# The first eleven stretches of an attention kernel in another written order, and its end with P V ahead of the output projection

## The chip, the cores and the metric

The kernel runs on one core of one Trainium2 chip, in one launch. The metric is the device time of one execution in microseconds: the median of 3 runs was 817.11 us before the change (814.79 to 817.4). A core has a matrix engine (TensorE, "PE" in the profile, its weight loads "PEld"), a vector engine (VectorE, "DVE"), a scalar engine for activations (ScalarE, "ACT"), a slower general engine (GpSimd, "POOL") and a queue that issues transfers (SyncE, "SP"). Each runs its own instructions in the order in which they were written; semaphores hold an instruction until what it reads is there and what it overwrites is free.

## The reference

```python
W = min(4096, max(256, Sk // 4))                                   # 512
q = (xn @ wq).reshape(B, Sq, Hq, Dh).transpose(0, 2, 1, 3)         # 2048 rows, 32 heads of 192
k = k_cache[:, :, Sk - W:, :];  v = v_cache[:, :, Sk - W:, :]
p = softmax(einsum("bhqd,bhkd->bhqk", q, k) * Dh ** -0.5)
s = einsum("bhqk,bhkd->bhqd", p, v).transpose(0, 2, 1, 3).reshape(B, Sq, Hq * Dh) @ wo
r = xn @ w_r;  idx = argsort(-r)[:, :2]                            # two tokens
y = (silu(x_sel @ w_gate) * (x_sel @ w_up)) @ w_down * sigmoid(r_sel)
g = silu(xn + scatter(y at idx))
return x + s * g                                                   # xn = layernorm(x), bfloat16
```

x is 2048 x 640, so 16 tiles of 128 rows. Nearly all the arithmetic is attention over the last 512 keys and the two projections around it; the feed-forward part touches two rows.

## The kernel before

The 32 heads go in 8 groups of 4, a group in two pairs of heads. A step i is one group, one block of 512 rows (t5, four tiles) and one pair: 64 steps, written i = 8g + 2·t5 + pair. A unit n is one tile of 128 rows of a step, n = 4i + u, so 256 units. Units are worked on in "stretches": stretches 0 and 1 have two units each, all others three, 86 in all (line 89).

What one stretch does is a list of tokens, read by `first` (line 636), each writing a few instructions:

- `S.j` (`scores`, L305 and L312): twelve matmuls into six PSUM tiles `sc`, two heads for each unit. The pool `ps_p` has six such buffers, so all of the last stretch's must be free.
- `M.n.h` (`row_max`, L320): the row maximum on DVE. `E.n.h` (`exps`, L327): the exponential on ScalarE, with the row sum. `P.n` (`p_turn`, L332): a transposing transfer of the probabilities, issued by SP.
- `q.i.c` (`q_mul`, L291): one of three 128-column parts of q for step i, five matmuls that read the turned activations `xnT` and the weights `wq_p` into a buffer of the pool `ps_f` (two buffers). `qe` (`q_out`, L281 on DVE or L283 on ScalarE) scales it out of PSUM. With a range of tiles behind it (`q.0.0.2.4`) only these rows are done.
- `R.j`, `O.n`, `OO.n.m`, `Oe.n` and `T.j`: for the stretch before, the reciprocal of the row sums, P V (`o_mul`, L346; in `ps_f` for `O`, in `ps_p` for `OO`), its scaling out of PSUM (`o_out`, L361 on DVE, L359 on ScalarE) and the transposing transfer of the result (`o_turn`, L367).
- `W.w` (`w_mul`, L394): the output projection of one tile of 128 rows for one group, twelve matmuls in two halves of 320 columns, from `oT` and `wo_g`, into two buffers of `ps_p`. `We.w` (`w_out`, L398 on) adds it to the sum `s_acc`; for the last group it multiplies by the gate and adds the rest (`fin_t`, L413 and `fin_o`, L415 or L419), and stores the tile. `OT.n` (`o_turn_pe`, L370 on) turns P V on TensorE in place of a transfer.
- Loads: `x` (x_in), `wq`, `k`, `kT` (a transposing transfer of k), `v`, `wo`. A trailing `a`, `v` or `g` names the engine (ScalarE, DVE, GpSimd); without one the transfer is issued by SP. (Where a range of tiles stands behind the letter, as in `qe.0.1.v.0.2`, the letter is not read and ScalarE does it.)
- Layer norm of a tile: `bn` (statistics on DVE) or `as` (the same on ScalarE, L223 and L224, with a small step on GpSimd), `rs.lo.hi.q` (the reciprocal root for tiles lo to hi in twelve Newton steps on DVE, L174 to L204) or `rg.lo.hi` (the same from the third step on GpSimd, fourteen steps, L191 to L210), `ap` (applying it), `turn` (turning on TensorE, copied out) or `xT.lo.hi` (a transposing transfer into `xnT`, L252).
- `B.j.k`: what the background plan has put into slot k of stretch j: the loads of later groups, the feed-forward part, the loads for the end.

The first ten stretches are written out by hand in the string `FIRST` (line 815), in which tokens of several stretches are mixed; stretches 10 to 84 come from `stretch(j)` (line 787) and the last from the string `LAST` (line 834). The scores of a stretch need q of its units: units 8 to 11 belong to step 2, which is the first to read tiles 4 to 7; step 4 reads tiles 8 to 11, step 6 tiles 12 to 15. The loads for the groups from 1 on are put by `at` (lines 719 to 732) a fixed number of units ahead of the group's first unit. A tile's buffer is reused in the order of the written release, and a transfer also waits until the one eight places earlier has landed.

## Time and profile before

| what | value |
|---|---|
| median of 3 runs | 817.11 us (814.79, 817.11, 817.4) |
| the profiled execution | 814.84 us |
| its span in the profile | 813.1 us |
| TensorE busy | 786.6 us (97%), 5742 matmuls |
| DVE busy | 630.7 us (78%) |
| ScalarE busy | 480.7 us (59%) |
| GpSimd busy | 168.1 us (21%) |
| data moved by transfers | 143.80 MB, mean 177 GB/s |
| mean granted TensorE clock | 0.992 |

The profile is of one execution. A row of a timeline has the start and the length of a run of like instructions, the engine, the line, the operation and its tiles, the count, and in brackets the idle time of that engine just before and what ended it. A row of the windows has the busy time of each engine within a stretch of time, the clock that TensorE was granted (1.00 is full), and what the 16 DMA engines did.

### The profile page before, as it was taken

How to read it: one execution, taken by the hardware profiler on the slowest of the kernel's cores; microseconds unless marked ns; L12 is line 12 of the kernel's file. 1: busy time of each engine (PE TensorE's matmuls, PEld its weight loads, DVE VectorE, ACT ScalarE, POOL GpSimd, SP SyncE). 2: the span in 40 equal slices, each digit the busy share in tenths (PEclk: the TensorE clock that was granted, in tenths of full speed). 3: DMA queues.
4: the chain of work that ended last, by engine and by line, in shares of the span. 5: the costliest groups of instructions: out<-in, count | busy, mean ns of one | idle time of the engine just before them, and what ended most of it. 6: DMA issues, size and time to landing. Idle time of an engine off the chain costs nothing.

```text
span 813.1 us, 15650 instructions
## 1 busy us (share of the span) xinstructions
PE 786.6 (97%) x5742; PEld 482.1 (59%) x5742; DVE 630.7 (78%) x1283; ACT 480.7 (59%) x1293; POOL 168.1 (21%) x185
## 2 busy tenths in 40 slices
...
GB/s 208 206 197 210 160 177 156 115 178 189 189 155 171 195 207 208 151 189 219 202 228 140 160 189 202 159 123 184 198 172 134 147 175 210 169 194 151 171 174 110
DMA packets 453005, 143.80 MB, mean 177 GB/s; under 512 B 422062, under 2 KB 452400, under 8 KB 452928
## 3 DMA queue, kind: packets, MB, share of 16 engines
...
q8 instruction: 45, 0.74, 0.4%
...
## 4 chain that ended last, share of the span: by engine, by line
PE 64%; DVE 3%; ACT 0%; issue 0%; DVEq 0%
PE w_ps L394 18%; PE q_ps L291 17%; PE o_ps L346 15%; PE sc L305 9%; PE sc L312 5%; DVE nm L320 1%; DVE xn L619 1%; DVE fin_t L413 0%; DVE fin_o L415 0%; ACT pexp L327 0%; PE gu_ps L558 0%; ACT qT L283 0%; DVE o_sb L361 0%; PE y_ps L595 0%; PE tp_o L379 0%
## 5 line engine op out<-in xcount | busy, mean ns | idle before, releaser
L327 ACT ACTIVATE pexp<-sc,nm 128x512 bf16<-128x512 f32 x512 | 348.4, 697 | 291.7 <-issue 244.3
L320 DVE TENSOR_REDUCE nm<-sc 128x1 f32<-128x512 f32 x512 | 314.9, 682 | 68.8 <-PE sc L312 68.8
L291 PE MATMUL q_ps<-xnT,wq_p 128*128 128x512 bf16 (+1 forms) x975 | 228.9, 380 | 15.5 <-DMA xnT<-xn 11.2
L394 PE MATMUL w_ps<-wo_g,oT 128*128 128x320 bf16 x1536 | 224.4, 300 | 2.4 <-ACT pexp L327 2.4
L394 PEld LDWEIGHTS <-oT 128*128 128x128 bf16 x1536 | 150.5, 98 | 74.9 <-issue 4.0
L346 PE MATMUL o_ps<-v_sb,pT 128*128 128x192 bf16 x2048 | 184.4, 246 | 0.0
L346 PEld LDWEIGHTS <-pT 128*128 128x128 bf16 x2048 | 171.6, 98 | 11.9 <-issue 1.4
L291 PEld LDWEIGHTS <-wq_p 128*128 128x128 bf16 x975 | 88.9, 98 | 142.4 <-issue 53.8
L361 DVE TENSOR_TENSOR o_sb<-o_ps,lsum 128x384 bf16<-128x384 f32 x247 | 136.6, 557 | 43.9 <-PE o_ps L346 24.7
L305 PE MATMUL sc<-kT,qT 128*128 128x512 bf16 x512 | 125.5, 379 | 1.5 <-ACT qT L283 1.0
L408 DVE TENSOR_TENSOR s_acc<-s_acc,w_ps 128x320 f32<-128x320 f32 x192 | 91.9, 483 | 32.6 <-PE w_ps L394 32.6
L327 ACT ACTIVATION_READ_ACCUMULATOR pexp<-sc,nm 128x1 f32 x512 | 110.2, 215 | 0.0
L283 ACT ACTIVATE qT<-q_ps 128x512 bf16<-128x512 f32 (+1 forms) x188 | 104.2, 607 | 4.5 <-PE q_ps L291 4.3
L305 PEld LDWEIGHTS <-qT 128*128 128x128 bf16 x512 | 48.7, 98 | 42.9 <-ACT qT L283 1.6
L312 PE MATMUL sc<-kT,qT 64*128 64x512 bf16 x512 | 70.2, 380 | 0.0
L632 POOL TENSOR_TENSOR s_acc<-s_acc,xn 128x640 f32<-128x640 f32 x16 | 22.4, 1403 | 113.4 <-DVE s_acc L408 113.3
L312 PEld LDWEIGHTS <-qT 64*128 64x128 bf16 x512 | 18.0, 94 | 46.7 <-issue 36.0
L611 POOL TENSOR_TENSOR xn<-xn,yh 128x640 bf16<-128x640 bf16 x32 | 44.7, 1395 | 2.7
...
L633 POOL TENSOR_TENSOR s_acc<-s_acc,x_fin 128x640 f32<-128x640 f32 x16 | 22.4, 1399 | 62.5 <-DMA x_fin<-in_A_x_dram 61.6
...
L610 POOL TENSOR_SCALAR yh<-y_bc,oh 128x640 bf16<-128x640 bf16 x32 | 25.7, 802 | 4.5 <-DMA y_bc<-y_d 3.0
...
## 6 DMA issues: line engine op xcount, KB each, us to landing
...
pT<-pexp SPq DMA_TRANSPOSE x256, 3.5
...
```

The lines of the kernel that those rows point to most:

```text
L283: nc.scalar.activation(out=out, in_=in_, func=ACT.Copy, scale=scale)
L291: nc.tensor.matmul(q_ps, lhsT=wq_of[g * PAIRS + pr][:, dc, c * P:(c + 1) * P], rhs=xnT[:, t5 * 4 + lo:t5 * 4 + hi, dc, :], start=(dc == 0) ...
L305: nc.tensor.matmul(sc_of[n][hh], lhsT=qT_of[i][:, 2 * hh, u * P:(u + 1) * P], rhs=kp[:, :, 2 * hh, :], start=True, stop=False)
L312: nc.tensor.matmul(sc_of[n][hh], lhsT=qT_of[i][hs, 1, u * P:(u + 1) * P], rhs=kp[hs, :, 1, :], start=False, stop=True)
L320: nc.vector.tensor_reduce(out=nm_of[j][:, c:c + 1], in_=sc_of[n][hh], axis=AX.X, op=ALU.max, negate=True)
L327: nc.scalar.activation(out=pe_of[n][:, hh, :], in_=sc_of[n][hh], func=ACT.Exp, bias=nm_of[j][:, c:c + 1], scale=1.0, accum_out=l_of[j][:, ...
L346: nc.tensor.matmul(ps[:, hh, :], lhsT=pT_of[n][:, hh, jj, :], rhs=v_sb[:, hh, jj, :], start=(jj == 0), stop=(jj == NJ - 1))
L361: nc.vector.tensor_tensor(out=osb_of[j][:, m], in0=ps, in1=l_of[j][:, 2 * m:2 * m + 2].unsqueeze(2).to_broadcast([P, 2, Dh]), op=ALU.mult)
L394: nc.tensor.matmul(w_ps, lhsT=oT_of[j][:, stretches[j].index(n), c % 3, :], rhs=wo_of[g][:, c, lo:hi], start=(c == 0), stop=(c == CPG - 1))
L408: nc.vector.tensor_tensor(out=acc, in0=acc, in1=w_ps, op=ALU.add)
L610: nc.gpsimd.tensor_scalar(out=yh, in0=M["y_bc"][:, j, :], scalar1=M["oh"][:, n, j:j + 1], scalar2=0.0, op0=ALU.mult, op1=ALU.add)
L611: nc.gpsimd.tensor_tensor(out=xn[:, n, :], in0=xn[:, n, :], in1=yh, op=ALU.add)
```

## The change

Four edits.

1. `FIRST` is written anew and now holds eleven stretches, 0 to 10 (`J0 = 11`). The tokens of a stretch are the same work; their order differs, some have another engine, and Newton steps, statistics and o_out are shared out otherwise.
2. The loads of group 1 are no longer placed by `at` (its loop begins at group 2) but are tokens in `FIRST`, with their own places; one of them, and the first load of tile 2, is issued from ScalarE's queue.
3. A stretch with no q left (only stretch 84) is written by a new function, `end_stretch`, with P V of the first two units ahead of the projections; `LAST` does the same for stretch 85.
4. The last tile's projection is done in three pieces of 320, 192 and 128 columns, each stored as soon as it is done; the tile before the last two goes to GpSimd; the last four tiles are stored from SP's queue.

```diff
@@ w_out
             if e == "v":
                 nc.vector.tensor_tensor(out=o[:, lo:hi], in0=t[:, lo:hi], in1=s_acc[:, n, lo:hi], op=ALU.add)
-        if e == "v":
-            nc.sync.dma_start(out=out_v[:, n, :], in_=o)
-        else:
+                if w == 4 * NS // PAIRS - 1:
+                    nc.sync.dma_start(out=out_v[:, n, lo:hi], in_=o[:, lo:hi])
+        if w == 4 * NS // PAIRS - 1:
+            return
+        if e == "g":
             nc.gpsimd.tensor_tensor(out=o, in0=t, in1=s_acc[:, n, :], op=ALU.add)
-            nc.gpsimd.dma_start(out=out_v[:, n, :], in_=o)
+        (nc.gpsimd if w < 4 * NS // PAIRS - 4 else nc.sync).dma_start(out=out_v[:, n, :], in_=o)
@@ first
-            w_mul(*n)
+            w_mul(*n, *([((0, HD), (HD, DA), (DA, D))] if n[0] == 4 * NS // PAIRS - 1 else []))
@@ the background plan
-    for g in range(1, NG):
+    for g in range(2, NG):
@@ new
+    def end_stretch(j):
+        a, b, c = stretches[j - 1]
+        out_ = ["R.%d" % (j - 1), "O.%d" % a, "O.%d" % b]
+        for k, w in enumerate(w_in[j]):
+            out_ += ["W.%d" % w]
+            if k == 0:
+                out_ += ["Oe.%d.v" % a, "B.%d.2" % j, "Oe.%d.v" % b]
+            if k == 1:
+                out_ += ["O.%d" % c]
+            out_ += ["We.%d.g" % w]
+        return out_ + ["Oe.%d.v" % c, "T.%d" % (j - 1), "B.%d.3" % j]
@@ stretch
+        if not qs:
+            return out_ + end_stretch(j)
@@ FIRST, the opening and stretches 0, 1, 2
-x.0.0.1 bn.0.0 x.0.1.2 bn.0.1 sq.0.1 bn.1.0 bn.1.1 rc.0.1 k.0.0 k.0.1 sq.1.2 ap.0.v kt.0.a rc.1.2 sx ap.1.v wq.0 turn.0.v turn.1.v x.0.2.3 kt.1.a x.0.3.4 q.0.0.0.2 q.0.2.0.2 qe.0.0.a.0.2 bn.3.0 q.0.1.0.2 bn.2.0 x.1.0.2 qe.0.2.v.0.2 bn.3.1 qe.0.1.v.0.2 bn.2.1 v.0 sq.2.4 rc.2.4 ex ap.3.v ap.2.v
-S.0 turn.3.v x.1.2.4 k.1.0 M.0.0 k.1.1 wq.1 turn.2.a M.1.0 E.0.0 q.0.0.2.4 qe.0.0.a.2.4 M.1.1 q.0.1.2.4 bn.7.0 E.1.0 E.1.1 qe.0.1.v.2.4 q.0.2.2.4 qe.0.2.a.2.4 as.5 kT.1 B.2.0 P.1 M.0.1 bn.7.1 bn.6.0 E.0.1
-S.1 bn.6.1 M.2.1 q.1.2 M.2.0 M.3.1 q.1.0 E.2.0 E.2.1 qe.1.2.a M.3.0 bn.4.0 qe.1.0.a bn.4.1 q.1.1 rs.4.8.0 rs.4.8.1 rs.4.8.2 rs.4.8.3 E.3.0 rs.4.8.4 rs.4.8.5 rs.4.8.6 v.1 rs.4.8.7 rs.4.8.8 E.3.1 rs.4.8.9 rs.4.8.10 rs.4.8.11 x.2.0.2 P.0 qe.1.1.a ap.5.v R.0
-S.2 P.2 M.5.0 P.3 x.2.2.4 ap.7.a M.4.0 O.0 M.5.1 ap.4.g ap.6.a as.9 bn.8.0 M.6.0 xT.4.6 M.4.1 bn.10.0 E.5.0 Oe.0.a bn.8.1 O.1 E.5.1 bn.11.0 bn.11.1 Oe.1.a bn.10.1 rs.8.12.0 B.2.3 rs.8.12.1 E.4.0 B.2.1 xT.6.8 rg.8.12 ap.11.g M.6.1 E.4.1 q.2.0 qe.2.0.a x.3.2.4 T.0 P.5 E.6.0 x.3.0.2 q.2.1 ap.8.v qe.2.1.a P.4 E.6.1 q.2.2 B.4.0 P.6 O.3 qe.2.2.a
+x.0.2.3.a x.0.0.1 x.0.1.2 bn.0.0 bn.1.0 bn.0.1 bn.1.1 sq.0.1 sq.1.2 rc.0.1 k.0.0 rc.1.2 k.0.1 ap.0.v ap.1.v x.0.3.4 sx wq.0 kt.0.a x.1.0.2 kt.1.a turn.0.v turn.1.a x.1.2.4 q.0.0.0.2 q.0.2.0.2 B.2.0 bn.2.0 qe.0.0.v.0.2 q.0.1.0.2 qe.0.2.v.0.2 bn.3.0 qe.0.1.v.0.2 bn.2.1 wq.1 bn.3.1 sq.2.4 bn.7.0 ex rc.2.4 ap.3.v k.1.0 ap.2.v
+S.0 turn.3.a M.0.1 M.0.0 turn.2.a E.0.0 q.0.0.2.4 bn.7.1 q.0.2.2.4 k.1.1 M.1.0 qe.0.0.v.2.4 M.1.1 E.1.0 v.0 q.0.1.2.4 bn.6.0 kT.1 bn.6.1 qe.0.2.a.2.4 qe.0.1.v.2.4 as.5 bn.4.0 x.2.0.2 v.1 bn.4.1 E.1.1 E.0.1 P.1
+S.1 M.2.0 E.2.0 M.2.1 q.1.2 x.2.2.4 rs.4.8.0 rs.4.8.1 E.2.1 rg.4.8 qe.1.2.a bn.8.0 bn.8.1 P.2 q.1.0 M.3.0 M.3.1 qe.1.0.a ap.7.g ap.5.v q.1.1 B.3.3 ap.4.v E.3.0 ap.6.v E.3.1 P.0 xT.4.6 qe.1.1.a
+S.2 R.0 M.4.0 M.5.0 bn.11.0 O.1 as.9 O.0 M.4.1 bn.11.1 E.4.0 as.10 xT.6.8 M.5.1 M.6.0 rs.8.12.0 rs.8.12.1 Oe.0.a E.4.1 E.5.0 Oe.1.a E.6.0 rg.8.12 R.1 P.3 q.2.0 M.6.1 qe.2.0.v q.2.1 x.3.2.4 q.2.2 B.4.0 B.2.1 qe.2.1.v B.2.3 P.4 ap.11.v T.0 E.6.1 P.6 O.2 E.5.1 qe.2.2.v
...
@@ FIRST, stretches 4, 5, 6
-S.4 Oe.6.a q.4.1 P.8 M.10.0 E.10.0 B.2.2 P.7 M.12.1 M.11.1 M.10.1 M.11.0 M.12.0 q.4.0 qe.4.1.a E.10.1 P.9 E.11.0 E.12.0 B.4.1 bn.15.0 OO.7.8 E.12.1 E.11.1 Oe.7.v O.9 qe.4.0.a T.2 P.10 as.14 wo.0.1 bn.15.1 Oe.8.v
-S.5 Oe.9.v M.13.0 P.11 M.14.1 T.3 B.3.2 E.13.0 P.12 B.6.1 M.14.0 rs.12.16.0 q.5.0 qe.5.0.a E.14.0 E.14.1 B.4.3 B.4.2 M.13.1 q.4.2 qe.4.2.v E.13.1 M.15.0 W.0 OO.10.11 P.14 rs.12.16.1 R.4 rs.12.16.2 rs.12.16.3 q.5.1 rs.12.16.4 rs.12.16.5 rs.12.16.6 rs.12.16.7 rs.12.16.8 rs.12.16.9 rs.12.16.10 E.15.0 P.13 rs.12.16.11 Oe.10.a ap.13.g Oe.11.a M.15.1 B.7.1 We.0.a ap.12.v O.12 ap.15.v E.15.1 ap.14.v qe.5.1.v
-S.6 xT.14.16 B.5.3 M.17.0 B.6.2 Oe.12.v M.16.0 P.15 B.6.0 xT.12.14 M.18.0 E.17.0 M.16.1 B.5.1 E.16.0 B.7.3 B.7.0 M.18.1 E.16.1 E.18.0 E.18.1 q.5.2 R.5 q.6.0 M.17.1 E.17.1 W.2 We.2.a B.5.2 qe.6.0.v OO.13.14 W.1 P.17 T.4 We.1.a Oe.13.v qe.5.2.a Oe.14.v O.15
+S.4 P.7 M.10.0 M.10.1 M.11.0 P.8 q.4.1 as.13 P.9 q.4.0 E.10.0 E.10.1 qe.4.1.a M.11.1 T.2 M.12.0 E.11.0 bn.15.0 R.3 E.11.1 wo.0.0 E.12.0 OO.7.8 M.12.1 P.10 B.4.1 B.7.2 E.12.1 O.9 as.14 Oe.7.v qe.4.0.a Oe.8.v
+S.5 B.3.0 bn.15.1 B.6.1 q.4.2 wo.0.1 B.5.3 Oe.9.v M.13.0 M.14.0 M.14.1 P.12 E.14.0 q.5.0 E.13.0 P.11 B.7.1 M.13.1 E.14.1 E.13.1 W.0 T.3 rs.12.16.0 qe.4.2.a P.14 qe.5.0.a rs.12.16.1 rs.12.16.2 rs.12.16.3 M.15.0 rs.12.16.4 rs.12.16.5 E.15.0 B.4.3 rs.12.16.6 rs.12.16.7 rs.12.16.8 rs.12.16.9 OO.10.11 q.5.1 rs.12.16.10 B.7.3 rs.12.16.11 P.13 ap.15.g O.12 ap.14.v B.6.2 B.5.1 ap.12.g B.6.3 R.4 M.15.1 Oe.10.v Oe.11.a qe.5.1.v We.0.a E.15.1
+S.6 Oe.12.a M.17.0 ap.13.g xT.14.16 q.5.2 xT.12.14 M.16.0 M.18.0 M.17.1 v.2 E.17.0 P.15 B.8.0 E.16.0 qe.5.2.v M.16.1 wo.1.0 E.18.0 E.16.1 R.5 B.7.0 k.2.0.a B.5.2 W.2 M.18.1 E.18.1 q.6.0 E.17.1 B.8.3 B.5.0 qe.6.0.a B.4.2 k.2.1 W.1 We.1.v OO.13.14 Oe.13.v We.2.a wq.2 Oe.14.v P.16 O.15
...
@@ FIRST, stretch 10 (before: written by stretch(10), without its own loads)
+S.10 B.9.3 M.28.0 q.8.2 M.29.0 E.28.0 M.28.1 q.9.0 M.30.0 E.28.1 P.27 M.29.1 R.9 E.29.0 W.9 E.29.1 wo.1.1 qe.8.2.v OO.25.26 E.30.0 P.28 O.27 B.8.1 M.30.1 Oe.25.a P.29 v.3 E.30.1 We.9.v Oe.27.v Oe.26.v qe.9.0.v W.8 T.8 We.8.v T.9 P.30 B.10.0
@@ LAST
-    S.85 M.253.0 M.253.1 E.253.0 E.253.1 P.253 M.254.0 M.254.1 E.254.0 E.254.1 P.254 M.255.0 M.255.1 E.255.0 E.255.1 P.255
-    B.85.0 W.120 We.120.g W.121 We.121.g R.84 O.250 Oe.250.v O.251 Oe.251.v O.252 Oe.252.v T.84 B.85.1 B.85.2 B.85.3
-    W.122 We.122.g W.123 We.123.g R.85 O.253 Oe.253.v O.254 Oe.254.v O.255 Oe.255.v W.124 We.124.g OT.253.a OT.254.a OT.255.a
-    W.125 We.125.v W.126 We.126.v W.127 We.127.v
+    S.85 B.85.0 M.253.0 M.253.1 E.253.0 E.253.1 P.253 M.254.0 M.254.1 E.254.0 E.254.1 P.254 M.255.0 M.255.1 E.255.0 E.255.1 P.255
+    R.84 O.250 O.251 W.120 W.121 Oe.250.v Oe.251.v O.252 We.120.g Oe.252.v We.121.g T.84 B.85.1 B.85.2 B.85.3
+    W.122 We.122.g W.123 We.123.g R.85 O.253 Oe.253.v O.254 Oe.254.v O.255 Oe.255.v OT.253.a W.124 We.124.g OT.254.a OT.255.a
+    W.125 We.125.g W.126 We.126.v W.127 We.127.v
```

Stretches 3, 7, 8 and 9 are reordered in the same manner. In stretches 7 to 9 and 10 stand the other loads of group 1: k.3 and wq.3 in stretch 8, kT.3 and, at its end, kT.2 in stretch 9, wo.1.1 and v.3 in stretch 10. Before, `at` had these in slots that the string put into stretches 6 to 10, and v.3 in stretch 12.

10 lines of the change are left out of this document (5 added, 5 removed).

## The prediction

> **What bounds the kernel now.** I read the page first, then the busy time by stage (cut where each stretch's first score matmul starts), then TensorE's own timeline, then the DMA-issuing queue's.
>
> ```profile
> span 813.1 us, 15650 instructions
> PE 786.6 (97%) x5742; PEld 482.1 (59%) x5742; DVE 630.7 (78%) x1283; ACT 480.7 (59%) x1293; POOL 168.1 (21%) x185
> ```
>
> TensorE is busy 786.6 of 813.1 us, so an order that leaves the work as it is can win 26.5 us of idle time at most, and whatever runs at a low clock. The stages say where that lies (columns: window, length, PE busy, PEld, DVE, ACT, POOL, granted clock, DMA share, GB/s):
>
> ```profile
> 22.56:37.13 14.57, 9.37 (x52) 4.57 (x51) 9.15 (x29) 11.28 (x29) 5.29 (x18) 0.77 1.04 210
> 37.13:46.15 9.02, 8.20 (x63) 4.84 (x61) 6.86 (x14) 5.83 (x17) 0.44 (x1) 1.00 0.87 179
> 46.15:52.80 6.65, 6.53 (x48) 3.67 (x47) 5.64 (x12) 6.55 (x19) 0.38 (x2) 1.00 1.16 167
> 52.80:62.08 9.28, 9.20 (x66) 5.33 (x64) 7.85 (x25) 9.25 (x27) 1.17 (x3) 1.00 1.00 202
> 62.08:80.08 18.00, 11.97 (x74) 6.65 (x71) 7.40 (x15) 6.67 (x19) 2.00 (x10) 0.81 1.08 208
> 80.08:117.80 37.72, 37.72 (x276) 23.40 (x274) 26.45 (x52) 24.04 (x65) 0.00 (x0) 1.00 0.88 169
> 117.80:778.03 660.23, 659.33 (x4854) 405.58 (x4853) 525.61 (x1043) 391.94 (x1060) 142.11 (x132) 1.00 0.95 176
> ```
>
> The rows are stretch 2, 3, 4, 5, 6, then 7 to 10, then 11 to 83. From stretch 7 to stretch 83 TensorE never rests for more than 0.9 us in all; nothing written there can be hurried. The loss is in stretch 2 (5.2 idle) and stretch 6 (6.0 idle), both at a reduced clock. Their rows in the timelines of TensorE, DVE and the SP queue, the landing times of the xnT transposes, and windows inside the two waits:
>
> ```profile
> 8.28 1.90 PE L291 MATMUL q_ps<-xnT,wq_p 128*128 128x256 bf16 x15 [1.26 <-DMA wq_p<-in_A_wq_dram]
> 31.40 5.24 PE L291 MATMUL q_ps<-xnT,wq_p 128*128 128x512 bf16 x15 [5.20 <-DMA xnT<-xn]
> 64.23 1.25 PE L291 MATMUL q_ps<-xnT,wq_p 128*128 128x512 bf16 x5
> 71.51 2.29 PE L291 MATMUL q_ps<-xnT,wq_p 128*128 128x512 bf16 x5 [6.03 <-DMA xnT<-xn]
> 73.60 3.03 PE L394 MATMUL w_ps<-wo_g,oT 128*128 128x320 bf16 x12
> 77.79 1.79 PE L394 MATMUL w_ps<-wo_g,oT 128*128 128x320 bf16 x12
> 25.35 3.48 SPq L252 DMA_TRANSPOSE xnT<-xn  x2
> 62.89 1.34 SPq L252 DMA_TRANSPOSE xnT<-xn  x1
> 60.83 0.16 DVE L204 SCALAR_TENSOR_TENSOR nmr<-mv,rstd 128x4 f32<-128x4 f32 x1
> 65.75 0.57 SPq L131 DMA_DIRECT2D wo_g<-in_A_wo_dram  x1
> 66.42 1.35 SPq L252 DMA_TRANSPOSE xnT<-xn  x1
> DMA to landing us min/median/max: 3.5/4.3/5.0
> 28.40:31.40 3.00, 0.00 (x1) 0.50 1.26 251
> 65.50:69.30 3.80, 0.00 (x0) 1.00 1.00 221
> 69.30:71.50 2.20, 0.00 (x0) 0.50 1.26 268
> ```
>
> Both times q_mul waits for the turned activations (xnT): of tiles 4 to 7 in stretch 2, of tiles 12 to 15 in stretch 6. The first wait begins at 26.20 and the clock is at 0.50 from 28.40, 2.2 us into it; the second begins at 65.50 and the clock holds for 3.8 us, to 69.30. It stays low for a while after each. Five q matmuls take 1.25 us at full clock; so the fifteen at 31.40 should take about 3.4 and took 5.24: 1.84 lost. At 71.51 five took 1.04 too long and twelve w_ps matmuls 3.03 in place of 1.79: 2.28 lost. The two stalls with what follows cost 7.0 and 8.3 us.
>
> **Stretch 2.** Before, DVE runs all twelve Newton steps of rstd for tiles 4 to 7; after, DVE does the first two and POOL the rest (rg.4.8), as it does before for tiles 8 to 11. The rows are the first and the last of the two kinds, and POOL's two applied tiles:
>
> ```profile
> 21.80 0.17 DVE L174 TENSOR_SCALAR nw_v<-mv 128x4 f32<-128x4 f32 x1
> 24.05 0.16 DVE L204 SCALAR_TENSOR_TENSOR nmr<-mv,rstd 128x4 f32<-128x4 f32 x1
> 31.85 0.20 POOL L191 TENSOR_TENSOR nw_a<-rstd 128x4 f32<-128x4 f32 x1 [4.87 <-DVE rstd L177]
> 35.52 0.20 POOL L210 TENSOR_SCALAR nmr<-nmr 128x4 f32<-128x4 f32 x1
> 35.83 1.75 POOL L239 TENSOR_SCALAR xn<-x_in,rstd,nmr 128x640 bf16<-128x640 bf16 x2
> 19.38 1.28 DVE L320 TENSOR_REDUCE nm<-sc 128x1 f32<-128x512 f32 x2
> ```
>
> On DVE the chain is 2.4 us (21.80 to 24.21); two steps on DVE and fourteen on POOL are 0.4 + 3.9 = 4.3. But it starts sooner: the statistics bn.4 now stand in stretch 0, and the chain follows the first two row maxima (end of the two before the row at 19.38, about 19.4) in place of all four and bn.4 (21.80). It ends at 19.4 + 4.3 = 23.7 rather than 24.2; the rstd that DVE needs is there two POOL steps (0.6) earlier, so three tiles on DVE and one on POOL (0.88) are done by 24.6, where ScalarE's second was done about 26. SP then issues the second transpose near 25.0 and not near 26.7 (25.35 and one issue of 1.35). Also x.2.2.4 no longer stands just ahead of the pair. At the 4.7 us that this transfer took (26.7 to 31.40) it lands at 29.7, at the median at 29.3: **1.8 us gained** (0.5 if POOL is late, 2.8 at the fastest landing, 3.5). About 3.4 us of idle time stay, between the 2.2 and the 3.8 at which the clock fell; I take half of the 1.84 back: **0.9** (0 to 1.84). POOL's own chain for tiles 8 to 11 (4.3 again) now stands, through ap.11.v, ahead of qe.2.2.v on DVE and so of stretch 3; fifteen q matmuls and O.2 take as long, which covers it. Without that cover it costs a microsecond, inside the 0.5.
>
> The Trainium skill, "TensorE: Matmul & The Clock Gate", Part 1, says that the array falls to half rate after at least one idle window of about 3.4 us, and that windows run free. This trace agrees with the half rate, but fell after 2.2 once. By the page the clock would mostly hold and the sum be 0.9 better.
>
> **The start and stretches 0 to 1.** wq.0 moves behind x.0.3.4 in SP's queue, x.0.2.3 goes to ScalarE's queue, turn.1 and turn.3 are copied by ScalarE. The first q matmul already waits 1.26 us for wq.0 (row at 8.28): a 160 KB transfer more ahead, but one queue more issuing. I take 0, from −0.4 to +0.8.
>
> **Stretches 3 to 5.** Here ScalarE is full: 6.55 of 6.65 and 9.25 of 9.28 us. The order takes one statistic (as.12) and one o_out off ScalarE and puts two q evictions on. But in stretch 4 as.13 now precedes the exponentials, and as.14 precedes qe.4.0, whose PSUM buffer q.4.2, the first product of stretch 5, takes over.
>
> ```profile
> 47.21 0.74 ACT L223 ACTIVATE junk_a<-x_in 128x640 bf16<-128x640 bf16 x1
> 48.90 0.71 ACT L359 ACTIVATE o_sb<-o_ps,lsum 128x192 bf16<-128x192 f32 x2
> ```
>
> One such statistic is 1.69 us (47.21 to 48.90). Behind it on ScalarE wait the exponentials, and TensorE for their PSUM. If both show they cost 3.4; the idle 1.0 us that these three stages now have (24.95 less 23.93 busy) is in reach too. I take **+1.2 lost** (−1.0 to +3.0).
>
> **Stretch 6.** Between the two transposes P.15 and the load wo.1.0 go away: the second can be issued at 62.89 + 1.34 = 64.2 and not at 66.42, **2.2 us sooner**, if its tiles are there: POOL now applies three of the four (0.88 each) behind the Newton steps, which before end at 61.0 (row at 60.83), so at 63.6. DVE is relieved of two of its three. w_mul(2), 1.63 us of work (twelve of the 24 matmuls that take 3.42 at the end, less the 1.79 of the other twelve), moves ahead of q.6.0. The 1.2 lost above lies ahead of this wait and behind the statistics, so it shortens the wait by as much. Left: 6.03 − 2.2 − 1.63 − 1.2 = 1.0. Under 2.2 idle the clock stays: the 2.28 go. w_mul(2) now waits for early exponentials to free PSUM, 0.4. Gain 5.0 + 2.28 − 0.4 = **6.9** (2 to 8.3). v.2, wo.1.0, k.2 and wq.2 all follow the transposes, so they share the engines as k and v do now. k.2.0 is issued from ScalarE between two exponentials; at 0.57, as the load at 65.75 took on SP, it makes the next ones that much later, and the exponentials end before stretch 7 needs them.
>
> **Stretches 7 to 10** have 37.72 of 37.72 busy and the same matmuls. kT.3, kT.2 and v.3 move; v.3 waits on SP for O.27 with T.8, T.9 and P.30 behind it. T.8 is late next: issued 0.6 after O.27 (one load's issue, as in the row at 65.75), it lands 3.5 to 5.0 later by the transposes above, 4.1 to 5.6 after O.27. w_mul(10) reads it behind w_mul(8) (1.63), ten q matmuls (two of 1.1) and stretch 11's scores, near 6 in all. Hidden by these: 0 (to +1.5).
>
> **The end.**
>
> ```profile
> 781.45 3.42 PE L394 MATMUL w_ps<-wo_g,oT 128*128 128x320 bf16 x24 [1.21 <-ACT pexp L327]
> 790.11 3.42 PE L394 MATMUL w_ps<-wo_g,oT 128*128 128x320 bf16 x24 [1.21 <-ACT pexp L327]
> 793.07 1.53 POOL L419 TENSOR_TENSOR fin_o<-fin_t,s_acc 128x640 bf16<-128x640 f32 x1 [3.86 <-DVE fin_t L413]
> 802.16 0.55 POOL L420 DMA_DIRECT2D out_dram<-fin_o  x1 [0.30 <-POOL fin_o L419]
> 803.45 0.33 PE L379 MATMUL tp_o<-ident,o_sb 128*128 128x128 bf16 x3 [0.40 <-ACT oT L380]
> 809.86 0.49 DVE L415 TENSOR_TENSOR fin_o<-fin_t,s_acc 128x320 bf16<-128x320 f32 x1
> DMA to landing us min/median/max: 1.8/2.1/2.7
> ```
>
> P V of two units fills each wait for pexp (2 × 1.21), and OT.253 earlier the 0.40: TensorE ends up to 2.8 sooner. DVE does not: its row maxima and o_out still precede We.120, so POOL's chain starts near 793.1 as now and tile 123 leaves at 802.2 plus 2.1 to 2.7, 804.3 to 804.9. Tile 126 takes its fin_o buffer (three in all). From 804.6 DVE has the last three steps of 126, the two of 127's first 320 columns, 0.49 each, and four for 192 and 128 columns, some 0.35 each: 3.9, so 808.5 against 810.35. **1.9 gained** (1.2 to 2.8). Of the rest: We.125 goes to POOL, which costs DVE two steps less and is not last; tiles 124 to 127 leave through SP, which has nothing else to issue by then; the third piece of w_mul(127) is six matmuls more on TensorE for the same columns, and in exchange the last store is 128 columns wide and not 640. I leave both ends of that inside the bounds. The rest of the span, 2.75 us from there to 813.1, stays.
>
> **Sum**, against the profiled execution's 814.84 us (span and 1.74 around it): −1.8 − 0.9 + 1.2 − 6.9 − 1.9 = −10.3, 804.5. The runs' median, 817.11, is 2.3 above the profiled execution; I put the new median 0.5 above the sum: **805.0**.
>
> **Rivals.** The clock holds and stretches 3 to 5 lose nothing: −10.3 − 0.9 − 1.2 = −12.4, 802.4; 801 if the landing is fastest too. For it: the wait of 3.8 at full clock. The second stall stays: one transpose 3 us later than I put it (three POOL tiles in a row, a landing of 5.0) leaves 4 idle and the 2.28: 5.3 back, 810. For it: 5.1 us from 66.42 to 71.51. ScalarE binds stretches 3 to 5 (+3.0) and T.8 is late (+1.5): 808. That it doesn't do what it says, stalls of the same length elsewhere: 815 to 819. And slower: the DMA engines bind. From stretch 2 to 11 they moved
>
> ```profile
> 22.56:117.80 95.24, 82.99 (x564) 48.46 (x562) 63.36 (x144) 63.62 (x171) 9.29 (x32) 0.93 0.97 187
> ```
>
> 187 GB/s, 17.8 MB; v.3 adds 0.4. To win 8.4 us there they need 18.2 MB in 86.8 us, 210 GB/s. At the 176 of stretches 11 to 83 it takes 103 us, 8 more than now, and the end gives back 2: 821. It decides below 187 GB/s. Against it: 210 and 208 GB/s in two stages above, and 251 and 268 inside the stalls.
>
> **Chances.** Forecast 0.45, second stall stays 0.18, ScalarE and T.8 0.12, clock holds 0.11, same 0.03, DMA-bound 0.11. 0.3%, 2.4 us, is what a measurement can tell from no change: faster 0.86, within 0.03, slower 0.11. The range, 798.5 to 812.5, takes in every case but the last two; the forecast's own is 802 to 808.
>
> **What would show it.** Right: q_ps waits for xnT about 3.4 us in stretch 2 and under 2 in stretch 6; the clock at 1.00 from stretch 6 on; stretch 7 starts near 72 (80.08 less 8.4); no wait of w_ps for pexp after 770. Wrong: waits for oT, pT or wq_p between stretches 7 and 11, or a wait in stretch 6 over 3 us with w_ps rows near 3.0.

## The result and the profile after

| | before | after |
|---|---|---|
| median of the runs made together | 815.68 us (6 runs) | 811.02 us (6 runs, 808.89 to 811.84) |
| ratio after / before | | 0.9939, 95% interval 0.9921 to 0.9957 |
| the profiled execution, its span | 814.84, 813.1 us | 810.83, 809.1 us |

The change gained 4.7 us between the medians and 4.0 between the two profiled executions; 10.3 was forecast. The first lines of the page of after, then its busy time by stage, cut as before where the first score matmul of stretch 2, 3, 4, 5, 6, 7 and 11 starts, and at stretch 84 (columns: window, length, PE, PEld, DVE, ACT and POOL busy, granted clock, DMA share, GB/s):

```profile
span 809.1 us, 15671 instructions
PE 786.4 (97%) x5748; PEld 481.9 (60%) x5748; DVE 626.4 (77%) x1267; ACT 480.4 (59%) x1299; POOL 173.3 (21%) x201
```

```profile
22.84:36.10 13.26, 9.20 (x52) 4.45 (x51) 8.36 (x20) 9.70 (x28) 6.38 (x21) 0.87 1.17 220
36.10:44.13 8.03, 8.03 (x61) 4.82 (x60) 6.94 (x16) 4.82 (x14) 0.00 (x0) 1.00 0.78 167
44.13:50.65 6.52, 6.46 (x50) 3.68 (x48) 5.49 (x11) 6.49 (x18) 0.19 (x1) 1.00 1.18 170
50.65:60.37 9.72, 9.31 (x66) 5.27 (x65) 8.42 (x27) 8.98 (x26) 2.64 (x4) 1.00 1.10 244
60.37:74.46 14.09, 11.36 (x72) 6.37 (x71) 6.57 (x13) 6.62 (x19) 2.24 (x11) 0.88 1.16 195
74.46:113.69 39.23, 37.93 (x275) 23.35 (x274) 24.02 (x47) 26.35 (x73) 0.00 (x0) 1.00 0.98 182
113.69:775.33 661.64, 659.81 (x4854) 405.63 (x4852) 525.20 (x1042) 391.65 (x1060) 141.87 (x132) 1.00 0.94 176
```

Against the rows of before: stretch 2 is 1.31 us shorter, stretches 3 to 5 together 0.68, stretch 6 3.91; stretches 7 to 10 are 1.51 longer, which before had no idle time at all, and 11 to 83, where the code is the same, 1.41. The start of stretch 2 is 0.28 later. From stretch 84 on it is 33.77 us (809.1 − 775.33) where it was 35.07, 1.30 less. Together −4.0.

TensorE's timeline of after has the stalls that remain (in brackets the idle time and what ended it):

```profile
30.71 4.90 PE L291 MATMUL q_ps<-xnT,wq_p 128*128 128x512 bf16 x15 [3.40 <-ACT o_sb L359]
56.02 1.38 PE L394 MATMUL w_ps<-wo_g,oT 128*128 128x320 bf16 x9 [0.41 <-DMA wo_g<-in_A_wo_dram]
63.95 1.79 PE L394 MATMUL w_ps<-wo_g,oT 128*128 128x320 bf16 x12 [0.19 <-ACT pexp L327]
68.28 2.31 PE L291 MATMUL q_ps<-xnT,wq_p 128*128 128x512 bf16 x5 [2.54 <-DMA xnT<-xn]
70.39 2.26 PE L394 MATMUL w_ps<-wo_g,oT 128*128 128x320 bf16 x12
92.08 0.83 PE L346 MATMUL o_ps<-v_sb,pT 128*128 128x192 bf16 x8 [1.30 <-DMA pT<-pexp]
```

The wait for xnT in stretch 6 is 2.54 us and not 1.0, and the rows behind it still run at a lowered clock (0.50 until 71.32; 2.31 and 2.26 us in place of 1.25 and 1.79, 1.5 lost). The wait at 92.08, in stretch 8, is new. What the queues did around the first of these, from the timelines of SP and GpSimd and from the transfers of 56 to 78 us (last column: median us from issue to landing):

```profile
60.11 3.07 SPq L252 DMA_TRANSPOSE xnT<-xn  x2
63.24 0.76 SPq L124 DMA_DIRECT2D v_sb<-in_A_v_cache_dram  x1
60.58 0.71 POOL L434 DMA_DIRECT2D wr_bc<-in_B_w_r_dram  x1
```

```profile
q0 software_dynamic: 48, 0.16, 6.8%
wr_bc<-in_B_w_r_dram POOLq DMA_DIRECT2D x1, 160.0 KB, 6.7
xnT<-xn SPq DMA_TRANSPOSE x2, 6.9
```

SyncE issued the second of the pair at 61.6 us, where 64.2 was forecast. The transposes landed after 7.2 and 6.6 us where they had taken 3.8 and 5.0. Among the transfers in flight beside them were v.2 and wr_bc, a row of 1,280 bytes that GpSimd's queue copies to 128 partitions; its 0.16 MB held 6.8% of 16 engines for 22 us.

### The profile page after: what moved, and what is told of

It is laid out like the page before. It is cut to its first block, busy times and chain, and to the rows that moved or that the text cites. A ratio compares the mean times of both kernels' runs of the same rounds, so it can differ in the third digit from the quotient of the medians.

```text
span 809.1 us, 15671 instructions
## 1 busy us (share of the span) xinstructions
PE 786.4 (97%) x5748; PEld 481.9 (60%) x5748; DVE 626.4 (77%) x1267; ACT 480.4 (59%) x1299; POOL 173.3 (21%) x201
## 5 line engine op out<-in xcount | busy, mean ns | idle before, releaser
L361 DVE TENSOR_TENSOR o_sb<-o_ps,lsum 128x384 bf16<-128x384 f32 x245 | 135.4, 557 | 48.3 <-PE o_ps L346 29.7
L283 ACT ACTIVATE qT<-q_ps 128x512 bf16<-128x512 f32 (+1 forms) x184 | 101.5, 606 | 3.8 <-PE q_ps L291 3.6
```

Source lines behind the costliest of these rows:

```text
L283: nc.scalar.activation(out=out, in_=in_, func=ACT.Copy, scale=scale)
L361: nc.vector.tensor_tensor(out=osb_of[j][:, m], in0=ps, in1=l_of[j][:, 2 * m:2 * m + 2].unsqueeze(2).to_broadcast([P, 2, Dh]), op=ALU.mult)
```

## The experiments

All start from the changed kernel except the first two. Stage lengths come from each kernel's profiled execution: the start of stretch 0; how long after the start of stretch 2 the first q matmul runs; stretch 2; stretch 6 with the landing times of its two transposes (where one figure stands, only the second's landing is in the trace); stretches 7 and 8; from stretch 85 to the end of the span. The last columns are the median of all runs and its ratio to the kernel before, run beside it (four sets, medians 815.3 to 816.6).

| kernel | S0 | q.2 | S2 | S6 | landing | S7 | S8 | end | median | ratio, 95% |
|---|---|---|---|---|---|---|---|---|---|---|
| before | 10.02 | 8.84 | 14.57 | 18.00 | 3.8, 5.0 | 9.55 | 9.61 | 26.41 | | |
| after | 11.04 | 7.87 | 13.26 | 14.09 | 6.6, 7.2 | 9.56 | 11.02 | 26.37 | 811.02 | 0.9921–0.9957 |
| c1_after | 11.59 | 7.95 | 13.53 | 14.17 | 5.6, 6.3 | 9.55 | 10.97 | 26.32 | 809.22 | 0.9901–0.9935 |
| e1_front | 11.00 | 6.46 | 12.33 | 11.39 | 5.3, 5.4 | 10.65 | 10.95 | 26.37 | 809.18 | 0.9904–0.9934 |
| e2_end | 10.52 | 8.67 | 15.03 | 18.34 | 4.0, 5.0 | 9.55 | 9.61 | 26.43 | 815.25 | 0.9979–0.9997 |
| e4_wr | 12.41 | 6.49 | 10.63 | 10.26 | 3.6 | 11.18 | 11.07 | 26.35 | 806.80 | 0.9871–0.9902 |
| e5_loads | 13.00 | 6.67 | 13.49 | 14.09 | 5.6, 6.2 | 9.55 | 11.66 | 26.29 | 812.07 | 0.9927–0.9967 |
| e3_p20 | 12.82 | 6.47 | 11.87 | 11.77 | 5.4, 5.8 | 10.41 | 9.56 | 26.39 | 806.89 | 0.9863–0.9898 |
| e10_p20_wr | 10.87 | 8.18 | 13.76 | 10.45 | 3.7 | 11.09 | 9.56 | 26.34 | 807.46 | 0.9888–0.9920 |
| e6_oe_dve | 11.92 | 7.10 | 12.61 | 12.34 | 5.4, 6.1 | 9.55 | 11.69 | 26.36 | 809.81 | 0.9907–0.9944 |
| e12_oe_first | 11.23 | 8.39 | 13.97 | 14.10 | 5.6, 6.6 | 9.56 | 10.93 | 26.30 | 810.12 | 0.9909–0.9936 |
| e13_v1 | 11.12 | 6.46 | 10.64 | 11.13 | 4.9, 5.4 | 10.33 | 10.86 | 26.37 | 807.84 | 0.9891–0.9931 |
| e7_bufs | 11.56 | 8.05 | 13.63 | 11.09 | 5.1, 5.1 | 11.07 | 10.32 | 26.35 | 808.44 | 0.9878–0.9911 |
| e9_stores | 11.55 | 8.09 | 13.67 | 11.50 | 5.4, 5.5 | 10.51 | 10.98 | 24.86 | 809.44 | 0.9878–0.9932 |
| e11_start | 10.56 | 6.42 | 10.63 | 10.96 | 4.7, 5.5 | 10.44 | 11.51 | 26.34 | 808.35 | 0.9885–0.9914 |
| e15_four | 10.03 | 6.78 | 12.36 | 10.17 | 3.7, 4.3 | 11.09 | 9.55 | 24.74 | 803.68 | 0.9839–0.9874 |
| e14_all | 11.63 | 6.65 | 12.23 | 10.41 | 3.9, 4.1 | 11.09 | 9.55 | 24.76 | 806.67 | 0.9862–0.9901 |
| e17_p16 | 10.91 | 7.95 | 14.24 | 10.49 | 3.8 | 10.69 | 11.09 | 26.29 | 808.81 | 0.9881–0.9916 |
| e16_six | 12.03 | 6.54 | 10.63 | 10.28 | 3.8 | 10.97 | 9.55 | 24.72 | 805.18 | 0.9846–0.9877 |

One profile is one draw: the first columns differ by microseconds between kernels whose order is the same up to there. So an edit is judged in its own stage and over all the profiles that share it.

**The halves of the change.** e1_front is the kernel before with the new `FIRST`, `J0` and loads; e2_end is the changed kernel with the old ones:

```diff
 e1_front, on the kernel before
-    for g in range(1, NG):
+    for g in range(2, NG):
...
-    J0 = 10
+    J0 = 11
...
```

> The kernel before with the new first eleven stretches and the new places of the second group's loads alone; the end is the old one. Theory (the two halves of the change add up, and the whole change got 4.0 us: about 2.7 by the start of stretch 84 and 1.3 in the end): stretch 12 starts near 121.6 us (before 125.72), stretch 84 takes 8.7 us as before, and the time stands 2.7 to 4.1 us under the kernel before, 4.1 if the 1.4 us that the middle gave back was only run to run. Rival (the middle gives back what the front gains): stretch 12 near 121.6 but stretch 84 again not before 775.3, so 2.7 us in all.

> The kernel before with the new end alone; the first stretches and the loads are the old ones. Theory: stretch 12 starts at 125.7 as before, stretch 84 takes 7.4 us in place of 8.66 (the waits for the exponentials are gone), and from the start of stretch 85 to the end of the span it takes the same 26.4 us as before, because VectorE's tail gives back what TensorE gained: 1.3 us under the kernel before. Rival (the tail of after is bad luck of one run): from stretch 85 to the end 24.6 us or less, and 3 us under the kernel before.

> The changed kernel itself, unaltered, once more beside the experiments, since its profiled run had stretches 2 and 6 at 13.26 and 14.09 us where two kernels with the same order up to there had 11.9 to 12.3 and 11.4 to 11.8. Theory (its profile shows one of the worse landings of the transposes, and they differ from run to run): stretch 6 takes 11.4 to 12 us in this profile, and the time of the five runs lies at 808 to 809 us, the new front (809.2) and the new end (0.6 less) added up. Rival (the two halves together have a stall that neither has alone): stretch 6 again near 14 us, and the median near 811.

e1_front reached stretch 12 at 119.23 us, 2.4 earlier than after did with the same order, and won 6.7 us: more than the whole change in its first run. e2_end gained 0.6 by the medians; its stretch 84 took 7.40 us in place of 8.66, and 26.43 us remained from stretch 85 on, as expected. The changed kernel run once more, unaltered, answered both ways: stretch 6 took 14.17 us again, so the first profile was no single bad one, yet the median came out at 809.22, with six runs from 807.19 to 813.08. The three with a mean granted clock of 0.992 or 0.993 took 809.57 to 813.08 us, the three with 0.995 to 0.997 took 807.19 to 808.88. So both halves gain, the end by little, and what the front gains differs from run to run. Stretches 12 to 83 take 652.1 to 654.2 us over all these profiles (before 652.31, after 653.71, e2_end 653.21): the 1.41 us there need not be the change's.

**Stretch 6: the broadcast, or the loads behind the transposes?**

```diff
 e4_wr
-        nc.gpsimd.dma_start(out=M["wr"], in_=B_w_r.partition_broadcast(P))
...
+    def m_wr():
+        nc.sync.dma_start(out=M["wr"], in_=B_w_r.partition_broadcast(P))
...
+    at(20, 5, m_wr)
...
 S.7 q.6.1 P.18
+B.7.5
 R.6
```

> The changed kernel with the load of wr_bc (one row of 1,280 bytes broadcast to 128 partitions) issued from SyncE in stretch 7, behind P.18, and no longer from GpSimd's queue at 60.58 us. Theory (this broadcast held the DMA engines from 62 to 66 us and made both transposes of xn slow): the two transposes of stretch 6 land after 3.8 to 5.2 us in place of 7.2 and 6.6, the wait before q.6.0 is under 0.9 us in place of 2.54, no slow clock follows, stretch 6 takes 10.2 to 11.5 us in place of 14.09, and stretch 12 starts near 118.5 us. Rival (v.2 and the other loads behind the transposes did it): the landings stay over 6 us and stretch 6 over 13 us. Third (the broadcast is slow wherever it stands): stretch 6 gains as above, and the transposes of stretch 7 or 8 land 2 us or more later, with a wait for pT of 1 us or more there.

```diff
 e5_loads
 S.6 M.17.1
-v.2
 E.17.0 P.15 B.8.0 E.16.0 qe.5.2.v M.16.1
-wo.1.0
...
 S.7 q.6.1 P.18
+v.2 wo.1.0
 R.6
```

> The changed kernel with the loads v.2 and wo.1.0 taken out of stretch 6 (issued at 63.24 and 67.07 us, behind the transposes of xn) and put into stretch 7, behind P.18. Theory that the broadcast of wr_bc alone slowed the transposes: they land after 5.3 us or more, as with the loads in place, and the wait before q.6.0 is 1.3 to 2.5 us. Rival (the loads slowed them): landings of 3.6 to 4.5 us, as with the broadcast moved, no wait before q.6.0 over 0.5 us, stretch 6 at 10.3 us.

The transfers of 56 to 78 us in e4_wr, its stretches 6, 7 and 8 by windows, and then the transposes in e5_loads:

```profile
wr_bc<-in_B_w_r_dram SPq DMA_DIRECT2D x1, 160.0 KB, 3.4
xnT<-xn SPq DMA_TRANSPOSE x2, 3.6
```

```profile
58.77:69.03 10.26, 9.89 (x73) 5.97 (x71) 6.68 (x13) 6.52 (x19) 1.87 (x10) 1.00 1.10 196
69.03:80.21 11.18, 10.06 (x72) 5.98 (x71) 5.46 (x10) 7.14 (x20) 0.00 (x0) 1.00 1.12 231
80.21:91.28 11.07, 9.73 (x72) 5.97 (x70) 5.46 (x10) 5.54 (x16) 0.00 (x0) 1.00 1.08 214
```

```profile
wr_bc<-in_B_w_r_dram POOLq DMA_DIRECT2D x1, 160.0 KB, 3.8
xnT<-xn SPq DMA_TRANSPOSE x2, 5.9
```

Without the broadcast there is no wait for xnT in stretch 6 at all and no slow clock. Without the two loads nothing changed. Over all profiles of the new order the split is complete: with wr_bc where the change has it, eleven profiles, 4.7 to 7.2 us; in the six with wr_bc moved, 3.6 to 4.3 (in four of them by the second transpose alone). So in this order the broadcast is what makes them slow. It is not enough that the two are in flight together, for they were so in the kernel before. GpSimd's row there, and the transfers of 61 to 66 us:

```profile
61.92 0.73 POOL L432 DMA_DIRECT2D wr_bc<-in_B_w_r_dram  x1
wr_bc<-in_B_w_r_dram POOLq DMA_DIRECT2D x1, 160.0 KB, 3.4
xnT<-xn SPq DMA_TRANSPOSE x1, 3.8
```

The first transpose, issued at 62.89, 0.97 us behind the broadcast, landed in 3.84 us there, and in 3.96 in e2_end. In the new order the first one is issued between 0.7 us ahead of the broadcast and 0.5 us behind it. What in this makes the difference, and whether the copying to 128 partitions or GpSimd's queue matters, was not tried apart: the one edit takes all of it away. Of the 3.8 us that stretch 6 gains over after, 1.6 return in stretch 7.

**Stretch 8: P.20 behind three loads.**

```diff
 e3_p20
 S.8 Oe.18.v
+P.20
 B.9.1 M.22.0 E.22.0 k.3.0 M.23.0 wq.3 R.7 q.7.0 q.7.1 M.22.1 M.24.0 E.23.0 k.3.1
-P.20
 M.23.1
```

> The changed kernel with the transpose P.20 issued at the head of stretch 8, ahead of the three loads k.3.0, wq.3 and k.3.1, where the changed order has it behind them. Theory (the place on the SyncE queue made the wait of 1.30 us for pT in stretch 8): no wait for pT over 0.3 us in stretch 8, which takes 9.6 us in place of 11.02, and the time 1.3 us under the changed kernel. Rival 1 (the loads themselves slow the transposes): the wait stays within 0.5 us of 1.30. Rival 2 (the stall moves): stretch 8 is 9.6 us, and a wait for kT, wq_p or pT of 1 us or more appears between stretch 9 and 12.

> Both moves that gained: P.20 at the head of stretch 8 and the load of wr_bc from SyncE in stretch 7. Theory (they are separate stalls): stretch 6 at 10.3 us, stretch 8 at 9.6 us and no wait for pT over 0.5 us there, and the time 1.3 to 1.5 us under the kernel with wr_bc alone moved (806.8), near 805.4. Rival (one of them only moves the other's stall): within 0.5 us of 806.8.

SyncE in after, then stretch 8 of e3_p20 by windows:

```profile
84.10 0.58 SPq L115 DMA_DIRECT2D k_raw<-in_A_k_cache_dram  x1
84.78 0.59 SPq L110 DMA_DIRECT2D wq_p<-in_A_wq_dram  x1
85.44 0.83 SPq L115 DMA_DIRECT2D k_raw<-in_A_k_cache_dram  x1
86.32 5.91 SPq L332 DMA_TRANSPOSE pT<-pexp  x3
```

```profile
83.16:92.72 9.56, 9.56 (x73) 6.02 (x71) 5.46 (x10) 5.54 (x16) 0.00 (x0) 1.00 1.21 211
```

With P.20 first, TensorE has no idle time in stretch 8: 9.55 or 9.56 us in all five profiles that have this edit, 10.32 to 11.69 in the twelve that do not. No wait of 1 us appeared in stretches 9 to 12 in its place. e10_p20_wr has both gains (stretches 6 to 8 take 31.10 us; e4_wr 32.51, after 34.67), but the time that was expected of it did not come: its stretch 2 took 13.76 us where e4_wr had 10.63.

**Stretch 2: ScalarE's queue, or the landing?** The row at 30.71 puts the wait down to ScalarE's o_out. Two edits were to free its buffers earlier, a third takes traffic away:

```diff
 e6_oe_dve
-Oe.0.a
+Oe.0.v
 E.4.1 E.5.0
-Oe.1.a
+Oe.1.v
```

> The changed kernel with the two evictions Oe.0 and Oe.1 of stretch 2 on VectorE and not on ScalarE, where they stand behind the statistics as.9 and as.10. Theory (the transposes of xn are the last to come, ScalarE's queue only ties with them): q.2.0 starts 6.3 us or more after the start of stretch 2, as in the profiles with quick landings (6.46 to 6.49; 7.87 in the changed kernel's first profile), and the time stays within 0.5 us of the changed kernel. Rival (ScalarE's queue sets it): q.2.0 starts under 5.8 us after the start of stretch 2, and the time falls by 0.7 to 2 us.

```diff
 e12_oe_first
 S.2 E.4.0
-as.10
 xT.6.8 M.5.1 M.6.0
+Oe.0.a Oe.1.a as.10
 rs.8.12.0 rs.8.12.1
-Oe.0.a
 E.4.1 E.5.0
-Oe.1.a
 E.6.0
```

> The changed kernel with the evictions Oe.0 and Oe.1 ahead of the statistics as.10 on ScalarE in stretch 2 (in the run with VectorE they stood behind its row maxima and were no earlier, so that it told nothing). Both buffers that q.2 needs are free about 5.6 us after the start of stretch 2. Theory (the transposes of xn are the last to come): q.2.0 still starts 6.3 us or more after the start of stretch 2 and waits for xnT. Rival (ScalarE's queue): it starts 5.6 to 6.0 us after, stretch 2 is at 10.5 to 12 us, and the time is 0.5 to 2 us under the changed kernel.

```diff
 e13_v1
 x.2.0.2
-v.1
 bn.4.1
...
 E.4.0 as.10 xT.6.8
+v.1
 M.5.1
```

> The changed kernel with the load v.1 (384 KB) taken out of stretch 1 and put behind the second transpose of xn in stretch 2. Theory (traffic ahead of the transposes of xn makes them late, and v.1 is its largest piece that nobody needs yet): q.2.0 starts 6.4 us or less after the start of stretch 2 (7.87, 7.95, 8.05, 8.09, 8.18 and 8.39 in the six profiles with late landings, 6.42 to 6.49 in four), stretch 2 takes 12 us or less, and the time is about 1.3 us under the changed kernel. Rival (what is late is not queued traffic but the landing itself, which differs from run to run): q.2.0 at about 8 us again.

The same row of TensorE in e12_oe_first and in e13_v1:

```profile
31.43 5.08 PE L291 MATMUL q_ps<-xnT,wq_p 128*128 128x512 bf16 x15 [3.71 <-DMA xnT<-xn]
```

```profile
29.39 3.69 PE L291 MATMUL q_ps<-xnT,wq_p 128*128 128x512 bf16 x15 [2.45 <-DMA xnT<-xn]
```

e6_oe_dve told nothing: its evictions stood behind VectorE's row maxima and ended at 31.95. e12_oe_first did: the buffers are free and TensorE waits longer still, for the transposes. ScalarE only ties with them. Why they are late in some profiles stays open. With v.1 behind them q.2 started after 6.46 and 6.65 us in both profiles (e13_v1, e14_all), but with v.1 ahead it did so too in seven of fourteen (6.42 to 6.78; e6_oe_dve aside), so two draws do not settle it. In e13_v1 stretch 3 took 9.04 us, a microsecond more than in every other profile of the new order, e14_all included (8.03 or 8.04).

**The end: a buffer, or GpSimd?**

```diff
 e7_bufs
-        fin_pool["o"] = pool("fin_o", 3)
+        fin_pool["o"] = pool("fin_o", 4)
```

> The changed kernel with four buffers in place of three for the output tile fin_o of the last group. In the changed kernel's first profile VectorE waits 0.80 us for the store of tile 123, and its next addition then takes 1.68 us in place of 0.49, until GpSimd's two additions end at 802.98. Theory (VectorE's addition is held while GpSimd works on the same kind of operands): the wait for out_dram is gone, the addition starts 0.8 us earlier but ends with GpSimd's all the same, taking about 2 to 2.5 us; from the start of stretch 85 to the end of the span 26.4 us, as before. Rival (the buffer is the cause of both): 0.49 us for that addition and 24.4 us for the end.

```diff
 e9_stores
-        (nc.gpsimd if w < 4 * NS // PAIRS - 4 else nc.sync).dma_start(out=out_v[:, n, :], in_=o)
+        (nc.gpsimd if w < 4 * NS // PAIRS - 7 else nc.sync).dma_start(out=out_v[:, n, :], in_=o)
...
 We.120.g Oe.252.v
-We.121.g
 T.84
+We.121.g
 B.85.1
```

> The changed kernel with the stores of tiles 121 to 123 issued from SyncE and not from GpSimd, where each stands 0.85 us between two additions (and T.84 ahead of We.121). Theory (GpSimd's chain of additions sets when VectorE's tail can run): GpSimd's last addition ends about 1.4 us earlier against the start of stretch 85 (18.8 us after it, where it was 20.25), VectorE's addition of tile 126 is over by then, and from stretch 85 to the end of the span it takes 24.8 to 25.2 us in place of 26.4. Rival (TensorE and VectorE's own work set it): 26.4 us within 0.3.

VectorE and GpSimd in after, in e7_bufs and in e9_stores:

```profile
800.38 0.49 DVE L413 TENSOR_TENSOR fin_t<-w_ps,xn 128x320 f32<-128x320 f32 x1 [0.39 <-PE w_ps L394]
801.66 1.68 DVE L415 TENSOR_TENSOR fin_o<-fin_t,s_acc 128x320 bf16<-128x320 f32 x1 [0.80 <-DMA out_dram<-fin_o]
799.38 0.55 POOL L422 DMA_DIRECT2D out_dram<-fin_o  x1 [0.30 <-POOL fin_o L421]
799.94 3.04 POOL L421 TENSOR_TENSOR fin_o<-fin_t,s_acc 128x640 bf16<-128x640 f32 x2
```

```profile
798.63 2.45 DVE L415 TENSOR_TENSOR fin_o<-fin_t,s_acc 128x320 bf16<-128x320 f32 x1
797.68 3.04 POOL L421 TENSOR_TENSOR fin_o<-fin_t,s_acc 128x640 bf16<-128x640 f32 x2
```

```profile
800.31 1.10 DVE L415 TENSOR_TENSOR fin_o<-fin_t,s_acc 128x320 bf16<-128x320 f32 x1
799.52 1.54 POOL L421 TENSOR_TENSOR fin_o<-fin_t,s_acc 128x640 bf16<-128x640 f32 x1 [0.42 <-POOL fin_o L421]
```

With a fourth buffer the wait is gone and the addition takes 2.45 us: it still ends 0.36 us after GpSimd's second one, and the end is 26.35 us. With three stores off GpSimd its chain ends 18.92 us after stretch 85 starts and not 20.25 (782.14 and 782.73 to 801.06 and 802.98), and the end falls by 1.5 us to 24.86. So GpSimd's chain sets the tail, not the buffer.

**The start.**

```diff
 e11_start
 rc.1.2 k.0.1
+wq.0
 ap.0.v ap.1.v x.0.3.4 sx
-wq.0
 kt.0.a x.1.0.2 kt.1.a turn.0.v
-turn.1.a
+turn.1.v
```

> The changed kernel with two pieces of the old start: wq.0 is issued ahead of x.0.3.4 and not behind it, and the copy of turn.1 is on VectorE. Theory (wq.0 behind more of x, and a copy on ScalarE, made the start late: stretch 0 began at 10.9 to 13.0 us in eight profiles of the new order, at 10.0 and 10.5 in the two of the old): stretch 0 starts at 10.0 to 10.6 us and stretch 2 at 22.0 to 22.5, so 0.3 to 2.5 us under the changed kernel. Rival (the landing of the first loads differs from run to run, whatever the order): stretch 0 starts at 11 us or later with a wait for wq_p or xnT over 1 us.

Stretch 0 began at 10.56 us here, and at 10.03, 11.63 and 12.03 in the three later kernels with this edit; without it at 10.87 to 13.00 in thirteen profiles. The two sets overlap: not settled.

**All together, and what comes next.** e15_four has the edits of e4_wr, e3_p20, e9_stores and e11_start; e14_all adds e13_v1 and two moves; e17_p16 is e4_wr with two transposes moved, e16_six e15_four with these and T.8 moved:

```diff
 e14_all
 M.12.1 P.10
+wo.0.1
 B.4.1 B.7.2
...
 q.4.2
-wo.0.1
 B.5.3
...
 S.10
+T.8
 B.9.3 M.28.0
...
 W.8
-T.8
 We.8.v
```

```diff
 e17_p16 and e16_six
 E.17.1
+P.16 P.17
 B.8.3 B.5.0 qe.6.0.a B.4.2 k.2.1
...
 wq.2 Oe.14.v
-P.16
 O.15
 S.7 M.19.0
-P.17
 M.20.0
```

```diff
 e16_six alone
 P.29
+T.8
 v.3
...
 W.8
-T.8
 We.8.v
```

> The changed kernel with the four edits that showed a gain in their own stretch: P.20 at the head of stretch 8, wr_bc from SyncE in stretch 7, the stores of tiles 121 to 123 from SyncE, and the start with wq.0 ahead of x.0.3.4 and turn.1 on VectorE. Theory (separate stalls, the sum): 1.4 (stretch 8) and 2 (stretches 6 and 7 together) and 1.5 (end) and 0.5 (start) under the changed kernel's 809 to 811, so 804 to 805. Rival (the stalls feed on one another, as P.20 and wr_bc together gave no more than wr_bc alone): 806.5 to 807.5.

> The kernel with those four edits and three more: v.1 behind the transposes in stretch 2, wo.0.1 in stretch 4 and not 5, and T.8 at the head of stretch 10. Theory: no wait for wo_g in stretch 5 (0.4 to 1.4 us in most profiles), none for oT in stretch 11, stretch 2 at 12 us or less; 802 to 804. Rival: wo.0.1 ahead slows the transposes of stretch 4 or 5, a wait for pT or xnT of 0.5 us or more appears there, and the time is that of the kernel with four edits or above.

> The kernel with wr_bc from SyncE in stretch 7, and P.16 and P.17 issued in stretch 6 ahead of the loads k.2.1 and wq.2, behind which SyncE reached them at 67.48 us and held them to 73.09. Theory (stretch 7 grows to 11.2 us when stretch 6 is short because ScalarE waits 2.01 us for the pexp buffer that these late transposes still read): the wait of ScalarE for pT is gone, stretch 7 takes 9.6 us, stretch 6 stays at 10.2 to 10.5, and the time is 1.5 us under the kernel with wr_bc alone moved (806.8). Rival 1 (ScalarE's own work is the bound there): stretch 7 stays at 11 us. Rival 2 (the loads that now come later are missed): a wait for wq_p or kT of 1 us or more in stretch 9 to 12.

> The kernel with the four edits (803.7 us), with P.16 and P.17 ahead of k.2.1 and wq.2 as above, and with T.8 ahead of the load v.3 in stretch 10, on which it waited. Theory (each is a stall of its own): stretch 7 at 9.6 us in place of 11.09, stretch 11 at 7.9 in place of 8.68, so 801 to 802. Rival (the next stall takes their place): 803 to 804, with a wait of 0.5 us or more for pT or oT in stretches 8 to 11 that the kernel with four edits does not have.

e15_four came to 803.68 us, 0.9856 of the kernel before: faster than both kernels, and its interval lies below that of c1_after. Its stretches 6 to 8 take 30.81 us and its end 24.74, both in their stages as expected. e14_all was no better (806.67): T.8 ahead of P.27 made a wait for pT of 2.25 us in stretch 10, and wo_g was still waited for 0.71 us with its load a stretch earlier. In stretch 7 the later kernels answer the question half. ScalarE in e4_wr, then TensorE in e16_six:

```profile
74.36 0.69 ACT L327 ACTIVATE pexp<-sc,nm 128x512 bf16<-128x512 f32 x1 [2.01 <-DMA pT<-pexp]
```

```profile
78.05 0.83 PE L346 MATMUL o_ps<-v_sb,pT 128*128 128x192 bf16 x8 [1.25 <-DMA pT<-pexp]
116.78 0.83 PE L346 MATMUL o_ps<-v_sb,pT 128*128 128x192 bf16 x8 [0.77 <-DMA pT<-pexp]
```

With P.16 and P.17 ahead of two loads ScalarE's wait is gone, but TensorE waits for another pT instead: stretch 7 takes 10.69 and 10.97 us, and SyncE still spent 5 us on the two. So ScalarE's work is not the bound, and the edit is no gain (e16_six 805.18, its ratio within e15_four's interval). In stretch 11 the wait for oT that e15_four had (0.59 us) is gone with T.8 ahead of v.3, and the 0.77 for pT takes its place.

## Why the prediction was wrong, step by step

| step | forecast | after | c1_after | what the runs showed |
|---|---|---|---|---|
| start, stretches 0 and 1 | 0 | +0.28 | +0.83 | at the edge of its bounds; up to +2.55 in another profile (e3_p20) |
| stretch 2 with its clock | −2.7 | −1.31 | −1.04 | xnT later than forecast, clock not held |
| stretches 3 to 5 | +1.2 | −0.68 | +0.23 | as.13 and as.14 did not show |
| stretch 6 | −6.9 | −3.91 | −3.83 | transposes slow with the broadcast at this place |
| stretches 7 to 10 | 0 | +1.51 | +1.45 | P.20 behind three loads |
| stretches 11 to 83 | 0 | +1.41 | +1.91 | differs from run to run |
| the end | −1.9 | −1.30 | −1.35 | addition held by GpSimd |
| sum | −10.3 | −4.0 | −1.8 | |

**Stretch 6 is the step that failed.** "The second can be issued at 62.89 + 1.34 = 64.2 and not at 66.42" was right; the pair was issued by 63.18. The term that was mis-sized is the landing: the sum kept the 5.0 us that the second transpose had taken before, and it took 6.6, with wr_bc, issued at 60.58, beside the pair. No term stood for what else is in flight at the new time. The 1.0 us left over became 2.54, and the clock fell in it, so "the 2.28 go" failed too: 1.5 of it stayed. The mechanism was right where the cause is taken away: in e4_wr stretch 6 takes 7.7 us less than before. The rival that came nearest in number, 810, was the second stall that stays. It had the transpose late by GpSimd's tiles and a landing of 5.0; the tiles were not late, the landing was longer still, and 2.54 us of idle time stayed and not 4, so that its number is near by luck.

**Stretches 7 to 10 failed outright.** "Hidden by these: 0 (to +1.5)" weighed only T.8 behind v.3. The change also moves P.20 behind k.3.0, wq.3 and k.3.1, in after 0.58 to 0.83 us of issuing each, and SyncE was 5.91 us in issuing the three transposes behind them. What the prediction gave as a sign of being wrong, a wait for pT between stretches 7 and 11, is the one that came. e3_p20 shows the price, 1.4 us against c1_after and 1.5 against after. T.8, which was named, cost nothing in after; once earlier stalls were gone TensorE waited 0.59 (e15_four) and 1.01 us (e11_start) for its oT in stretch 11.

**Stretch 2** had the right mechanism and the wrong size. The prediction read the old second transpose as issued at 26.7 and landing after 4.7 us. Its row of the timeline holds both issues, and the first took 2.03 us, not 1.35: the second was issued at 27.48 and landed after 3.78. After the change it was issued at 25.82, 1.7 us sooner as forecast, but landed after 4.76, so that only 0.7 of this was left. The landing was put at 29.7; q.2 started at 30.71. The wait for xnT that "what would show it" gave as about 3.4 us is 3.40. Half of the slow clock's 1.84 was to come back; 0.34 did (4.90 for 5.24). The two lengths at which the clock had fallen, 2.2 and 3.8 us, were no bounds for this: what counts is where a wait lies on the grid described at the end.

**Stretches 3 to 5** were forecast too dark: a full ScalarE there was not the bound. What takes part of the gain is a wait for wo_g in stretch 5, 0.41 us in after and 1.32 in c1_after, that before did not have and the prediction did not name. The 1.2 us that did not get lost also did not shorten the wait of stretch 6, as the sum had them do: for both steps together −5.7 was forecast and −4.59 came.

**The end** was right on the waits for pexp (none is left after 770) and on GpSimd's chain. With stretch 84 starting 2.70 us earlier than before, 2.70 has to be added to compare: tile 123's store was issued at 799.38, so 802.08, for 802.2 forecast, and VectorE could go on at 801.66, so 804.36, for 804.6. The step "DVE has the last three steps of 126, the two of 127's first 320 columns, 0.49 each" failed: the first of these took 1.68.

Of the 6.3 us that are missing, stretch 8's 1.4 and the end's 0.6 are shown by undoing them; in stretch 6 undoing the broadcast gives more than was missing there (3.8 us, of which 1.6 come back in stretch 7); the 1.41 of the middle and the 1.4 of stretch 2 are not tied to an edit.
